# Turning q and k of three sequences by 32x32 block transposes on VectorE, from loads in blocks of 32 tokens

## Chip, core and metric

The kernel is one program on one core of a Trainium2 chip. Its time is the device time of one execution in microseconds (us). Engines are named as the profile names them: PE is TensorE's matmuls and PEld its weight loads, DVE is VectorE, ACT is ScalarE, POOL is GpSimd, SP is SyncE, from whose queue all loads and stores are issued.

## What is computed

An attention in two parts over q, k, v of shape (4 sequences, 8 heads, 576 tokens, 64), and two gated layers of 2304 tokens behind it. The reference, cut:

```python
def _attn_ref(q, k, v):                       # factor = 4, scale = 1/8
    q_d, k_d, v_d = mean over groups of 4 tokens of q, k, v
    out_d = sm_attn(q_d, k_d, v_d)            # softmax attention of 144 pooled tokens
    out_up = np.repeat(out_d, factor, axis=2)
    mask = np.abs(pos[:, None] - pos[None, :]) < factor
    scores = np.where(mask, scale * q @ k.T, -1e9)
    out_local = softmax(scores) @ v           # each token sees 7 neighbours
    return out_up + out_local

x = attn_out as (2304, 512)
h = x @ w_in;  x = (h * sigmoid(h)) @ w_out              # layer 1, 512 -> 2048 -> 512
h = x @ w2_in; out = (h * sigmoid(1.702 * h)) @ w2_out   # layer 2, the same sizes
```

The four weight arrays come as 64-bit floats.

## The kernel before

**Attention.** Two heads fill the 128 partitions, so a sequence b has 4 head pairs (hp); a half of it (288 tokens) of one head pair is a unit u, and there are 32 units. m = u // 4 is the half-sequence, 0 to 7, and b = m // 2. For each head pair of a sequence `keys_of` makes the keys: the load brings k with tokens on 96 partitions (`kraw`, two DMAs, one per head), step KT (line 1101) turns it by six TensorE transposes of fp32 against an identity into the PSUM tile `kps`, KC (line 1104, ACT) copies it to SBUF as `kT`, and KD (line 1108, DVE) sums groups of four tokens from `kps` into `kd`. For each unit, `unit` does the same with q: QT (line 1134, three transposes into `qps`), QC (line 1138, ACT, into `qT`), QD (line 1142, DVE, into `qd`). Then follow the scores SC (lines 1153 and 1159, PE, into `sl`), the softmax (LC, LS, LE, LU, LN on DVE, ACT and POOL), the transposes TP of the pooled part (line 1213, PE), a 32x32 block transpose PT of the local weights on DVE (line 1221), and the products AV with v (lines 1230 and 1236, PE). `kps` takes the tag pa2 (one PSUM buffer, shared with `sl` and a part of AV), `qps` the tag pa1 (two, shared with TP and the rest of AV). The raw tiles `kraw` and `qraw` have two buffers each.

**Layers.** The 64-bit weights of layer 1 are loaded, rebuilt as fp32 by integer steps (lines 323 to 348, the last of them, cp at line 348, a sum that stands on DVE or on POOL) and split into two fp16 parts (hi, line 376, ACT; lo, line 380, DVE). Layer 1 multiplies 12 matmuls of 288 columns per output tile: `hps` (line 691), and `ops` (line 836 for m = 0, line 808 for m = 1 to 7). Layer 2 works on blocks of 256 tokens (lines 870 and 949).

**The order.** Every piece of work is a step of a plan. The order of all steps is a table, `PLACES`: two digits per step give its place, and the steps are issued in that order on each engine's queue, where they run strictly one behind the other. The table `ON` says for some steps on which of two engines they stand: cp of layer 1 (DVE or POOL), LS and LN (the subtraction of the maximum and the scaling, lines 1182 and 1206, DVE or POOL), gs2 (sums in layer 2, lines 889 to 891, DVE or POOL). Units of the attention are threaded between the matmuls of layer 1: while layer 1 works on half-sequence m - 1 or m - 2, the units of m are made.

The transposes that the change is about, as they stand:

```python
            for c in range(2 * NBL):
                nc.tensor.transpose(T[kps][:, c // NBL, (c % NBL) * TT:(c % NBL + 1) * TT], kr[:, c].rearrange("p h d -> p (h d)"), T["ident"][:TT, :TT])
```

## Time and profile before

| | us |
|---|---|
| median of 3 runs | 930.73 (927.39 to 931.24) |
| the profiled execution | 930.08 |
| its span, first to last instruction | 928.3 |
| PE busy in the span | 866.0 (93%) |
| DVE busy | 620.6 (67%) |
| ACT busy | 474.5 (51%) |
| POOL busy | 155.6 (17%) |

The profiled execution lies 0.65 us under the median; 1.8 us of it lie outside the span. Busy shares are means over stages that differ, so the stages are read apart: the weights of layer 1 are rebuilt up to about 155 us, the attention and layer 1 share the engines up to 554 us, and layer 2 fills the rest.

### The profile page before, as it was taken

How to read it: one execution, taken by the hardware profiler on the slowest of the kernel's cores; microseconds unless marked ns; L12 is line 12 of the kernel's file. 1: busy time of each engine (PE TensorE's matmuls, PEld its weight loads, DVE VectorE, ACT ScalarE, POOL GpSimd, SP SyncE). 2: the span in 40 equal slices, each digit the busy share in tenths (PEclk: the TensorE clock that was granted, in tenths of full speed). 3: DMA queues.
4: the chain of work that ended last, by engine and by line, in shares of the span. 5: the costliest groups of instructions: out<-in, count | busy, mean ns of one | idle time of the engine just before them, and what ended most of it. 6: DMA issues, size and time to landing. Idle time of an engine off the chain costs nothing.

```text
span 928.3 us, 23669 instructions
## 1 busy us (share of the span) xinstructions
PE 866.0 (93%) x10156; PEld 709.0 (76%) x10156; DVE 620.6 (67%) x1350; ACT 474.5 (51%) x835; POOL 155.6 (17%) x180
## 2 busy tenths in 40 slices
...
GB/s 212 240 270 180 130 127 72 71 107 138 98 134 71 106 116 202 32 165 53 105 79 253 43 91 1 12 13 1 24 2 23 24 24 1 13 2 35 1 23 24
DMA packets 87388, 77.02 MB, mean 83 GB/s; under 512 B 66036, under 2 KB 72692, under 8 KB 86260
## 3 DMA queue, kind: packets, MB, share of 16 engines
...
## 4 chain that ended last, share of the span: by engine, by line
PE 63%; DVE 26%; ACT 4%; POOL 2%; issue 2%; DMA 1%; SPq 0%; POOLq 0%; ACTq 0%; DVEq 0%
PE hps L691 19%; PE ops L808 17%; PE oy L949 8%; DVE g L898 7%; PE hps L870 5%; PE oz L949 4%; DVE tg L885 3%; DVE tg L890 2%; PE ox L949 2%; PE ul L1236 2%; DVE wout L380 1%; PE sl L1159 1%; ACT g L895 1%; DVE tg L889 1%; DVE tg L891 1%
## 5 line engine op out<-in xcount | busy, mean ns | idle before, releaser
L691 PE MATMUL hps<-xhl,win 128*128 128x288 f16 x1536 | 204.0, 292 | 3.6 <-DVE tg L706 3.6
L870 PE MATMUL hps<-xhl,win 128*128 128x256 f16 x1728 | 191.4, 273 | 1.2 <-DVE tg L885 1.1
L870 PEld LDWEIGHTS <-win 128*128 128x128 f16 x1728 | 169.0, 98 | 22.0 <-issue 2.5
L691 PEld LDWEIGHTS <-win 128*128 128x128 f16 x1536 | 150.4, 100 | 44.2 <-issue 4.7
L808 PE MATMUL ops<-g,wout 128*128 128x288 f16 x1344 | 171.9, 286 | 0.0
L949 PEld LDWEIGHTS <-g 128*128 128x128 f16 x1512 | 146.5, 98 | 27.7 <-DVE g L898 8.5
L808 PEld LDWEIGHTS <-wout 128*128 128x128 f16 x1344 | 129.8, 98 | 32.5 <-issue 0.6
L882 ACT ACTIVATE tg<-hps,blk 128x512 f32<-128x512 f32 x72 | 49.2, 684 | 102.5 <-PE hps L870 99.1
L895 ACT ACTIVATE g<-tg 128x896 f16<-128x896 f32 x72 | 67.4, 945 | 49.3 <-DVE tg L891 25.4
L898 DVE SCALAR_TENSOR_TENSOR g<-tg,g 128x896 f16<-128x896 f32 x72 | 77.6, 1087 | 19.4 <-ACT g L895 19.3
L885 DVE SCALAR_TENSOR_TENSOR tg<-tg,hps 128x512 f32<-128x512 f32 x72 | 49.2, 683 | 54.6 <-ACT tg L882 54.6
L949 PE MATMUL oy<-wout,g 128*128 128x256 f16 x648 | 75.1, 272 | 0.0
L889 POOL TENSOR_TENSOR tg<-tg 128x128 f32<-128x128 f32 x17 | 8.5, 502 | 387.4 <-DVE tg L885 362.6
L348 POOL TENSOR_TENSOR cs<-cs,cz 128x512 int32<-128x512 int32 x32 | 42.1, 1327 | 135.0 <-DVE cz L336 54.3
L706 DVE SCALAR_TENSOR_TENSOR tg<-tg,hps 128x576 f32<-128x576 f32 x64 | 47.7, 748 | 23.5 <-ACT tg L703 23.1
L703 ACT ACTIVATE tg<-hps,blk 128x576 f32<-128x576 f32 x64 | 47.2, 737 | 31.1 <-PE hps L691 24.3
L713 ACT ACTIVATE g<-tg,gs 128x576 f16<-128x576 f32 x56 | 42.7, 770 | 17.5 <-DVE tg L706 17.5
L927 ACT ACTIVATE o<-oy,blk 128x256 f32<-128x256 f32 x27 | 12.8, 473 | 74.1 <-PE oy L949 74.1
L716 DVE SCALAR_TENSOR_TENSOR g<-tg,gs,g 128x576 f16<-128x576 f32 x56 | 46.9, 847 | 5.1 <-ACT g L713 5.0
L323 ACT ACTIVATE st<-st 128x512 f32<-128x512 f32 (+1 forms) x48 | 39.2, 824 | 6.2 <-DMA st<-in_moe_w_in_dram 5.9
L933 DVE SCALAR_TENSOR_TENSOR o<-oy,blk,o 128x256 f32<-128x256 f32 x9 | 4.4, 484 | 54.6 <-PE oy L949 39.4
L949 PE MATMUL oy<-wx,g 128*128 128x256 f16 x216 | 29.3, 273 | 5.1 <-DVE g L898 4.3
...
## 6 DMA issues: line engine op xcount, KB each, us to landing
...
qraw<-in_q_dram SPq DMA_DIRECT2D x64, 72.0 KB, 3.9
kraw<-in_k_dram SPq DMA_DIRECT2D x32, 144.0 KB, 5.0
...
```

What stands on the lines that cost most here:

```text
L691: nc.tensor.matmul(o, T[w][:, kc, a, fc * P:(fc + 1) * P], T[xk][:, kc, b, :T_], start=(n == 0), stop=(n == 3 * KC - 1))
L703: ACT.activation(out=T[tg], in_=T[ps][:, :, :T_], func=AF.Tanh, scale=T["a" + bk][:, c:c + 1])
L706: DVE.scalar_tensor_tensor(out=T[tg], in0=T[tg], scalar=1.0, in1=T[ps][:, :, :T_], op0=ALU.add, op1=ALU.mult)
L713: ACT.activation(out=T[g][:, 0], in_=T[tg], func=AF.Copy, scale=gs)
L716: DVE.scalar_tensor_tensor(out=T[g][:, 1], in0=T[tg], scalar=gs, in1=T[g][:, 0], op0=ALU.mult, op1=ALU.subtract)
L808: nc.tensor.matmul(o, w[:, j, a, dc * P:(dc + 1) * P], g[:, b, j % 2, :], start=(n == 0), stop=(n == 3 * NF - 1))
L870: nc.tensor.matmul(o, T[w][:, kc, a, fc * P:(fc + 1) * P], T[xk][:, kc, b, :], start=(n == 0), stop=(n == 3 * KC - 1))
L882: ACT.activation(out=four(), in_=T[ps][:, 0, :], func=AF.Tanh, scale=T["a" + bk][:, c:c + 1])
L885: DVE.scalar_tensor_tensor(out=four(), in0=four(), scalar=1.0, in1=T[ps][:, 0, :], op0=ALU.add, op1=ALU.mult)
L895: ACT.activation(out=T[g][:, 0], in_=T[tg], func=AF.Copy, scale=GS2)
L898: DVE.scalar_tensor_tensor(out=T[g][:, 1], in0=T[tg], scalar=GS2, in1=T[g][:, 0], op0=ALU.mult, op1=ALU.subtract)
L949: nc.tensor.matmul(T[bank[acc]], g[:, a, slot, :], w, start=first and p == p0 and i == 0, stop=prod in (2, 3, 4) and p == NF // 2 - 1 and ...
```

## The change

For m >= 2, that is for the sequences 1, 2 and 3 (24 of 32 units, 12 of 16 key tiles), q and k are no longer turned on TensorE. `load_tokens` loads them in four DMAs instead of two, each for one head and one half of its 64 features: 32 partitions get the tokens with the same number modulo 32, and in each partition stand blocks of 32 features, one block for each 32 tokens. A run in memory is then 32 numbers (128 bytes) where it was 64 (256 bytes). One DVE transpose of 32x32 blocks (QX, KX) turns such a tile into `qT` or `kT`; `qd` and `kd` are summed from these SBUF tiles instead of PSUM. QT, QC, KT and KC are gone for these units, and with them their PSUM tiles. `qT` loses its padding: it is 288 + 8 columns, and the scores read 32 columns from every 24th. Sequence 0 keeps the old way. Both tables are new: `PLACES` holds a new order of all steps, and in `ON` six more of the sums cp stand on POOL (12 of 16, before 6), four more of LS, three more of LN, and five fewer of the layer 2 sums gs2.

```diff
@@ -23,13 +23,14 @@
 ON = {
-    "DVE": ("sg1.in.0.2 sg1.in.1.0 sg1.in.2.2 sg1.out.1.0 sg1.out.1.2 sg1.out.2.0 sg1.out.2.2 LS0 LN1 LS2 LN2 LS3 LS5 LS7 "
...
-    "POOL": ("cp1.in.0.2 cp1.out.0.0 cp1.out.0.2 cp1.out.1.2 cp1.out.2.0 cp1.out.2.2 gs2.1.7 gs2.4.7 gs2.6.7 gs2.8.7"),
+    "DVE": ("sg1.in.0.0 sg1.in.0.2 sg1.in.1.0 sg1.in.3.0 sg1.in.3.2 sg1.out.0.0 LS1 LN1 LS2 LN3 LS6 LS8 LN12 LS15 LN16 LN18 "
...
+    "POOL": ("cp1.in.0.2 cp1.in.1.2 cp1.in.2.0 cp1.in.2.2 cp1.out.0.0 cp1.out.0.2 cp1.out.1.0 cp1.out.1.2 cp1.out.2.0 "
+             "cp1.out.2.2 cp1.out.3.0 cp1.out.3.2"),
 }
@@ -42,47 +43,46 @@
 PLACES = (
-    "0007020a03080S010U1d0o1n1K1h050b0Y1O1Z090z0M0K0Q0O0W040n0p0I0s0P1i0C131b1c1s1z1U1f1M261T2q1V2I161E1R1J1X2e2o1L2f2u2j2y2m2Q1Y2D2M2L2T2R"
...
+    "00070301040908020W1g0h1j1W1q0F0G181F200b0y0C0N0H0P100d0T1a121k141n0c0I0Y0S150V1f0l171e1b1s1d1z111D1M1H1R1N1Y1C2a2o2g2A2k2P2n2V32353839"
...
@@ -1002,9 +1002,9 @@
         for t in T["kTs"]:
             POOL.memset(t[:, 0:BAND], 0.0)
             POOL.memset(t[:, BAND + S:], 0.0)
-        T["qTs"] = [ac.tile([P, 4 * NBL, 32], F32, name=f"qT{i}") for i in range(2)]
+        T["qTs"] = [ac.tile([P, HALF + 32 - QB], F32, name=f"qT{i}") for i in range(2)]
         for t in T["qTs"]:
-            POOL.memset(t, 0.0)
+            POOL.memset(t[:, HALF:], 0.0)
         T["smr"] = [ac.tile([P, 8], F32, name=f"smr{i}") for i in range(2)]
         for t in T["smr"]:
             POOL.memset(t, 1.0)
@@ -1019,21 +1019,35 @@
 
     NU = NM * NHP
 
+    def blocked(m):
+
+        return m >= 2
+
+    def load_tokens(t, src, n, blocks):
+
+        for hh in range(2):
+            if blocks:
+                for j in range(D // 32):
+                    q = 2 * hh + j
+                    nc.sync.dma_start(out=t[32 * q:32 * q + 32, :n].rearrange("p (c e) -> p c e", e=32),
+                                      in_=src[hh].rearrange("(c p) d -> p c d", p=32)[:, :, 32 * j:32 * j + 32])
+            else:
+                nc.sync.dma_start(out=t[:TT].rearrange("p (c h d) -> p c h d", h=2, d=D)[:, :, hh], in_=src[hh].rearrange("(c p) d -> p c d", p=TT))
+
     def load_kv(b, hp):
         h = slice(2 * hp, 2 * hp + 2)
         nm = f"{b}.{hp}"
 
         def lk():
-            T["kraw" + nm] = pools["ld"].tile([TT, 2 * NBL, 2, D], F32, tag="kraw", name="kraw")
-            for hh in range(2):
-                nc.sync.dma_start(out=T["kraw" + nm][:, :, hh], in_=k[b, 2 * hp + hh].rearrange("(c p) d -> p c d", p=TT))
+            T["kraw" + nm] = pools["ld"].tile([P, S + 2 * TT], F32, tag="kraw", name="kraw")
+            load_tokens(T["kraw" + nm], [k[b, 2 * hp + hh] for hh in range(2)], S, blocked(2 * b))
 
         def lv():
             T["vraw" + nm] = pools["ld"].tile([PD, 4, BAND * D], F32, tag="vraw", name="vraw", bufs=1)
             nc.sync.dma_start(out=T["vraw" + nm], in_=v[b, h].rearrange("h (c p r) d -> p (h c) (r d)", p=PD, r=BAND))
 
         n0 = len(plan.steps)
-        add("lk" + nm, "SP", 0.44, lk, w=["kraw" + nm], alloc=[("kraw", "kraw" + nm)], mb=0.69, nd=2)
+        add("lk" + nm, "SP", 0.44, lk, w=["kraw" + nm], alloc=[("kraw", "kraw" + nm)], mb=1.0 if blocked(2 * b) else 0.69, nd=4 if blocked(2 * b) else 2)
         add("lv" + nm, "SP", 0.36, lv, w=["vraw" + nm], alloc=[("vraw", "vraw" + nm)], mb=0.33)
         if b:
             for s in plan.steps[n0:]:
@@ -1045,11 +1059,10 @@
         qk = f"qraw{u}"
 
         def f():
-            T[qk] = pools["ld"].tile([TT, NBL, 2, D], F32, tag="qraw", name="qraw")
-            for hh in range(2):
-                nc.sync.dma_start(out=T[qk][:, :, hh], in_=q[b, 2 * hp + hh, half * HALF:(half + 1) * HALF].rearrange("(c p) d -> p c d", p=TT))
-
-        add("lq" + qk, "SP", 0.44, f, w=[qk], alloc=[("qraw", qk)], mb=0.35, nd=2)
+            T[qk] = pools["ld"].tile([P, HALF + TT], F32, tag="qraw", name="qraw")
+            load_tokens(T[qk], [q[b, 2 * hp + hh, half * HALF:(half + 1) * HALF] for hh in range(2)], HALF, blocked(m))
+
+        add("lq" + qk, "SP", 0.44, f, w=[qk], alloc=[("qraw", qk)], mb=0.5 if blocked(m) else 0.35, nd=4 if blocked(m) else 2)
 
     def load_vw(b, hp):
 
@@ -1096,17 +1109,21 @@
 
         def tr():
             T[kps] = bank2("kps")
-            kr = T["kraw" + nm]
+            kr = T["kraw" + nm][:TT].rearrange("p (c h d) -> p c (h d)", h=2, d=D)
             for c in range(2 * NBL):
-                nc.tensor.transpose(T[kps][:, c // NBL, (c % NBL) * TT:(c % NBL + 1) * TT], kr[:, c].rearrange("p h d -> p (h d)"), T["ident"][:TT, :TT])
+                nc.tensor.transpose(T[kps][:, c // NBL, (c % NBL) * TT:(c % NBL + 1) * TT], kr[:, c], T["ident"][:TT, :TT])
 
         def cpy():
             ACT.copy(out=T["kTs"][hp][:, BAND:BAND + S].rearrange("p (c t) -> p c t", c=2), in_=T[kps][:, :, :HALF])
 
+        def turn():
+            DVE.transpose(out=T["kTs"][hp][:, BAND:BAND + S], in_=T["kraw" + nm][:, :S])
+
         def pool():
             T[kd] = pools["at"].tile([P, 2 * PD], F32, tag="kd", name="kd", bufs=NHP)
+            src = T["kTs"][hp][:, BAND:BAND + S].rearrange("p (c e) -> p c e", c=2) if blocked(2 * b) else T[kps][:, :, :HALF]
             DVE.tensor_reduce(out=T[kd].rearrange("p (c t) -> p c t", c=2),
-                              in_=T[kps][:, :, :HALF].rearrange("p c (t r) -> p c t r", r=BAND), axis=AX.X, op=ALU.add)
+                              in_=src.rearrange("p c (t r) -> p c t r", r=BAND), axis=AX.X, op=ALU.add)
 
         def sv():
             T[vd] = pools["at"].tile([PD, 4, D], F32, tag="vd", name="vd", bufs=NHP)
@@ -1114,9 +1131,12 @@
             POOL.tensor_tensor(out=vr[:, :, 0:2, :], in0=vr[:, :, 0:2, :], in1=vr[:, :, 2:4, :], op=ALU.add)
             POOL.tensor_tensor(out=T[vd], in0=vr[:, :, 0, :], in1=vr[:, :, 1, :], op=ALU.add)
 
-        add("KT" + nm, "PE", 0.85, tr, r=["kraw" + nm, "init"], w=[kps], alloc=[("pa2", kps, 2 * NHP * b + hp - 0.1)])
-        add("KC" + nm, "ACT", act(S), cpy, r=[kps], w=[kT], alloc=[("kT" , kT)])
-        add("KD" + nm, "DVE", dve(S), pool, r=[kps], w=[kd], alloc=[("kd", kd)])
+        if blocked(2 * b):
+            add("KX" + nm, "DVE", dve(S), turn, r=["kraw" + nm, "init"], w=[kT], alloc=[("kT", kT)])
+        else:
+            add("KT" + nm, "PE", 0.85, tr, r=["kraw" + nm, "init"], w=[kps], alloc=[("pa2", kps, 2 * NHP * b + hp - 0.1)])
+            add("KC" + nm, "ACT", act(S), cpy, r=[kps], w=[kT], alloc=[("kT" , kT)])
+        add("KD" + nm, "DVE", dve(S), pool, r=[kT if blocked(2 * b) else kps], w=[kd], alloc=[("kd", kd)])
         add("KV" + nm, "POOL", 2.1, sv, r=["vraw" + nm], w=[vd], alloc=[("vd", vd)])
 
     def unit(u):
@@ -1131,15 +1151,19 @@
         def qtr():
             T[qps] = bank1("qps")
             for c in range(NBL):
-                nc.tensor.transpose(T[qps][:, c * TT:(c + 1) * TT], T[f"qraw{u}"][:, c].rearrange("p h d -> p (h d)"), T["ident"][:TT, :TT])
+                nc.tensor.transpose(T[qps][:, c * TT:(c + 1) * TT], T[f"qraw{u}"][:TT, c * 2 * D:(c + 1) * 2 * D], T["ident"][:TT, :TT])
 
         def qcp():
             T[qT] = T["qTs"][u % 2]
-            ACT.copy(out=T[qT][:, :, 0:QB], in_=T[qps][:, :HALF].rearrange("p (s a) -> p s a", a=QB))
+            ACT.copy(out=T[qT][:, :HALF], in_=T[qps][:, :HALF])
+
+        def turn():
+            T[qT] = T["qTs"][u % 2]
+            DVE.transpose(out=T[qT][:, :HALF], in_=T[f"qraw{u}"][:, :HALF])
 
         def qpl():
             T[qd] = pools["at"].tile([P, PD], F32, tag="qd", name="qd")
-            DVE.tensor_reduce(out=T[qd], in_=T[qps][:, :HALF].rearrange("p (t r) -> p t r", r=BAND), axis=AX.X, op=ALU.add)
+            DVE.tensor_reduce(out=T[qd], in_=T[qT if blocked(m) else qps][:, :HALF].rearrange("p (t r) -> p t r", r=BAND), axis=AX.X, op=ALU.add)
 
         def scores():
 
@@ -1156,7 +1180,7 @@
                     k0 = QB * (4 * (half * NBL + bl) + i)
                     for hh in range(2):
                         r = slice(D * hh, D * hh + D)
-                        nc.tensor.matmul(T[sl][32 * i:32 * i + 32, hh, bl * 32:bl * 32 + 32], T[qT][r, 4 * bl + i, :],
+                        nc.tensor.matmul(T[sl][32 * i:32 * i + 32, hh, bl * 32:bl * 32 + 32], T[qT][r, QB * (4 * bl + i):QB * (4 * bl + i) + 32],
                                          T["kTs"][hp][r, k0:k0 + 32], start=True, stop=True, tile_position=(D * hh, 32 * i))
 
         def sd():
@@ -1253,9 +1277,12 @@
         def xmax():
             DVE.tensor_reduce(out=small(L1, m, 10 + hp), in_=T[X][:, hp, :], axis=AX.X, op=ALU.max, apply_absolute_value=True)
 
-        add(f"QT{u}", "PE", 0.43, qtr, r=[f"qraw{u}", "init"], w=[qps], alloc=[("pa1", qps, u - (0.6 if hp else 0.05))])
-        add(f"QC{u}", "ACT", act(HALF), qcp, r=[qps], w=[qT], alloc=[("qT", qT)])
-        add(f"QD{u}", "DVE", dve(HALF), qpl, r=[qps], w=[qd], alloc=[("qd", qd)])
+        if blocked(m):
+            add(f"QX{u}", "DVE", dve(HALF), turn, r=[f"qraw{u}", "init"], w=[qT], alloc=[("qT", qT)])
+        else:
+            add(f"QT{u}", "PE", 0.43, qtr, r=[f"qraw{u}", "init"], w=[qps], alloc=[("pa1", qps, u - (0.6 if hp else 0.05))])
+            add(f"QC{u}", "ACT", act(HALF), qcp, r=[qps], w=[qT], alloc=[("qT", qT)])
+        add(f"QD{u}", "DVE", dve(HALF), qpl, r=[qT if blocked(m) else qps], w=[qd], alloc=[("qd", qd)])
         add(f"SC{u}", "PE", 1.1, scores, r=[qT, qd, kT, kd], w=[sl], alloc=[("mm", sl, sl_at[u]) if u < NHP else ("pa2", sl, u)])
         add(f"DM{u}", "DVE", dve(4 * PD) + 0.2, dmax, r=[sl], w=[nmx])
         add(f"LC{u}", "DVE", 2 * dve(192), lcap, r=[sl, "cap"], w=[sc], alloc=[("sc", sc)])
```

Where the instructions stand, at three places. First PE, in the stage in which attention and layer 1 run together, around the transposes of one key tile and one unit of sequence 2 (`hps` is layer 1, `kps` and `qps` are the transposed tiles, `tps` the pooled part of the unit ahead). Before:

```order
L691 LDWEIGHTS win_2_705
L691 MATMUL hps<-xhl,win_2_705 128x288
L1101 MATMUL kps<-ident,kraw 128x96 x6
L1134 MATMUL qps<-ident,qraw 128x96 x3
L1213 MATMUL tps<-ident,pd 72x72 x4
L691 LDWEIGHTS win_3_1080
```

After, at the scores of the same unit:

```order
L691 LDWEIGHTS win_3_916
L691 MATMUL hps<-xhl,win_3_916 128x288
L1177 MATMUL sl<-kd,qd 72x144 x2
L1183 MATMUL sl<-kT_150,qT_160 32x32 x24
L691 LDWEIGHTS win_3_916
```

The nine transposes are gone from PE's row, and layer 1 stands directly on both sides of the scores.

Second DVE, at the first key tile of sequence 1, with what each instruction waits for. Before:

```order
L1254 TENSOR_REDUCE blk<-xf 128x1
L1142 TENSOR_REDUCE qd<-qps 128x72 [waits PE_49]
L1108 TENSOR_REDUCE kd<-kps 128x144 [waits PE_49]
L764 TENSOR_REDUCE blk<-rm 128x1 [waits PE_49]
L336 TENSOR_SCALAR z<-st_1053 128x1024 [waits DMAHW4_49,Activation_49]
```

After:

```order
L1245 STREAM_TRANSPOSE PT<-sc 128x192 [waits Pool_49]
L1120 STREAM_TRANSPOSE kT_148<-kraw 128x576 [waits DMAHW6_49,DMAHW7_49,DMAHW1_49,DMAHW0_49]
L1227 TENSOR_TENSOR pd<-pd,smr_165 72x288 [waits DVE_49]
L1125 TENSOR_REDUCE kd<-kT_148 128x144 [waits DVE_49]
L1197 TENSOR_TENSOR sc<-sl,cap 128x192 [waits PE_49]
L1200 TENSOR_REDUCE mx<-sc 128x6 [waits DVE_49]
```

The block transpose of `kraw` now stands in DVE's own row and waits there for four DMAs; the scaling of `pd` and the rest of the softmax of an earlier unit queue behind it.

Third POOL, while the output weights of layer 1 are rebuilt (`x_80<-x_80,z` is the sum cp, `sc<-sc,mx` is LS and `sc<-sc,smr` is LN, `vraw` and `vd` are the pooling of v). Before:

```order
L348 TENSOR_TENSOR x_80<-x_80,z 128x1024 [waits DVE_49,PE_49]
L348 TENSOR_TENSOR x_80<-x_80,z 128x1024 [waits DVE_49,PE_49,Activation_49]
L1182 TENSOR_TENSOR sc<-sc,mx 128x192 [waits DVE_49,Pool_49]
L348 TENSOR_TENSOR x_80<-x_80,z 128x1024 [waits DVE_49,PE_49]
L1114 TENSOR_TENSOR vraw<-vraw 72x4x128 [waits DMAHW3_49]
```

After:

```order
L1132 TENSOR_TENSOR vd<-vraw 72x256 [waits PE_49,Pool_49]
L348 TENSOR_TENSOR x_80<-x_80,z 128x1024 [waits Activation_49]
L348 TENSOR_TENSOR x_80<-x_80,z 128x1024 [waits DVE_49,Activation_49]
L1206 TENSOR_TENSOR sc<-sc,mx 128x192 [waits DVE_49]
L1230 TENSOR_TENSOR sc<-sc,smr_164 128x192 [waits DVE_49]
L348 TENSOR_TENSOR x_80<-x_80,z 128x1024 [waits Activation_49]
```

The sums now come in pairs, four times in this stretch, and LS and LN of the units in work queue behind them.

## Rows read from the trace of the kernel before

**Rows 1.** Windows: stretch and length, each engine's busy us, clock, DMA share, GB/s

```profile
0.00:100.00 100.00, 60.33 (x1075) 40.59 (x1076) 80.47 (x186) 69.59 (x119) 31.80 (x45) 0.98 0.89 224
100.00:155.00 55.00, 45.37 (x664) 34.34 (x662) 53.89 (x121) 44.94 (x80) 22.55 (x16) 0.94 0.53 113
155.00:554.00 399.00, 396.10 (x5139) 314.29 (x5138) 268.57 (x643) 215.75 (x442) 72.38 (x69) 1.00 0.39 108
554.00:929.00 375.00, 364.17 (x3286) 319.81 (x3283) 217.66 (x403) 144.17 (x196) 28.88 (x51) 1.00 0.04 14
```

**Rows 2.** Chain of waits, two pieces: start us, us, what ran on the path

```profile
149.43 2.64 DVE wout L380 x2
...
536.27 17.65 PE ops L808 x144
```

**Rows 3.** Timeline of PE, 211 to 219 us: start us, us (ends modelled), instruction, count

```profile
211.10 4.58 PE L808 MATMUL ops<-g,wout 128*128 128x288 f16 x36
215.52 0.66 PE L1101 MATMUL kps<-ident,kraw 96*128 96x96 f32 x6
216.02 3.11 PE L808 MATMUL ops<-g,wout 128*128 128x288 f16 x24
```

**Rows 4.** Timeline of PE, 163 us: one unit's transposes between layer 1 matmuls

```profile
163.35 0.41 PE L1134 MATMUL qps<-ident,qraw 96*128 96x96 f32 x3
163.60 1.64 PE L691 MATMUL hps<-xhl,win 128*128 128x288 f16 x12
```

**Rows 5.** Windows of line 1134 (q transposes) alone: PE, PEld, clock, DMA

```profile
100.00:155.00 55.00, 2.09 (x12) 1.35 (x12) 0.94 0.53 113
155.00:554.00 399.00, 8.43 (x60) 6.80 (x60) 1.00 0.39 108
```

**Rows 6.** Windows of line 1101 (k transposes) alone, same columns

```profile
100.00:155.00 55.00, 2.75 (x24) 2.25 (x24) 0.94 0.53 113
155.00:554.00 399.00, 5.33 (x48) 4.62 (x48) 1.00 0.39 108
```

**Rows 7.** Groups of instructions: line, engine, operation, shapes, count | busy us, mean ns | idle before

```profile
L348 POOL TENSOR_TENSOR x<-x,z 128x1024 int32<-128x1024 int32 x6 | 15.3, 2555 | 17.9 <-ACT tg L703 5.6 <-DVE z L336 4.6 <-PE kps L1101 4.4
...
L1142 DVE TENSOR_REDUCE qd<-qps 128x72 f32<-128x288 f32 x32 | 14.5, 452 | 13.0 <-PE qps L1134 11.2 <-ACT qT L1138 1.5
...
L348 DVE CUSTOM_DVE_ANT_0 x<-x,z 128x2048 uint16<-128x2048 uint16 x10 | 12.0, 1209 | 0.0
L1108 DVE TENSOR_REDUCE kd<-kps 128x144 f32<-128x576 f32 x16 | 12.0, 751 | 10.8 <-PE kps L1101 9.6 <-ACT kT L1104 1.0
L1221 DVE STREAM_TRANSPOSE PT<-sc 128x192 f32<-128x192 f32 x32 | 11.9, 371 | 1.1 <-POOL sc L1206 0.8
...
L1206 DVE TENSOR_TENSOR sc<-sc,smr 128x192 f32<-128x192 f32 x16 | 8.4, 528 | 0.2
...
L1182 DVE TENSOR_TENSOR sc<-sc,mx 128x192 f32<-128x192 f32 x14 | 5.3, 377 | 0.3
```

**Rows 8.** Timeline, all engines, 96 to 106 us: a POOL sum and one DVE form twice

```profile
96.89 3.17 POOL L348 TENSOR_TENSOR x<-x,z 128x1024 int32<-128x1024 int32 x1 [4.62 <-DVE z L336]
...
98.98 1.70 DVE L716 SCALAR_TENSOR_TENSOR g<-tg,g 128x576 f16<-128x576 f32 x1 [1.14 <-ACT g L713]
...
105.07 0.75 DVE L716 SCALAR_TENSOR_TENSOR g<-tg,g 128x576 f16<-128x576 f32 x1
```

**Rows 9.** DMA queue, 0 to 5 us: packets, MB, share of 16 engines

```profile
q1 hardware_dynamic: 2367, 0.60, 53.3%
```

**Rows 10.** DMA queue, 117 to 127 us, same columns

```profile
q1 hardware_dynamic: 4613, 1.35, 96.8%
```

**Rows 11.** DMA issues of the page: form, count, KB each, median us to landing

```profile
qraw<-in_q_dram SPq DMA_DIRECT2D x64, 72.0 KB, 3.9
kraw<-in_k_dram SPq DMA_DIRECT2D x32, 144.0 KB, 5.0
```

**Rows 12.** Timeline of SP, 231 us: four issues in one row

```profile
231.08 1.97 SPq L1067 DMA_DIRECT2D vw<-in_v_dram  x4
```

79 lines of the change are left out of this document (39 added, 40 removed), and 10 rows, old and new, of the table ON.

## The prediction

> **What bounds the kernel now.** I read the windows first, because the page's shares are means over three unlike stages. Up to 155 us DVE is the full engine, 53.89 of the last 55 us, while PE has 45.37 [rows 1]; the chain of waits runs there through DVE's splits of the weights [rows 2]. From 155 to 554 us PE is busy 396.10 of 399 us, DVE 268.57 and ACT 215.75 [rows 1], and the chain is PE's own matmuls [rows 2]. Modelled ends can make PE look fuller than it is, so I check the starts: 36 matmuls of layer 1 from 211.10 to 215.52 are 123 ns each, with nothing between them [rows 3]. PE is then truly the bound, and what leaves its row comes off the end, as long as nobody else gets late. From 554 us on PE has 364.17 of 375 us [rows 1] and no attention is left.
>
> **What PE loses.** The duration of one transpose says little, since they overlap; the start of the next instruction says it. Six transposes of a key tile hold PE from 215.52 to 216.02, 0.50 us [rows 3]; three of a unit hold it from 163.35 to 163.60, 0.25 us [rows 4]. In the PE-bound stage stand 60 transposes of q [rows 5] and 48 of k [rows 6], that is 20 units and 8 key tiles, and all belong to sequences 1 to 3. So the stage gets shorter by 20 x 0.25 + 8 x 0.50 = 5.0 + 4.0 = 9.0 us. The other 4 units and 4 key tiles (12 transposes of q, 24 of k) stand from 100 to 155 us, where PE has 9.6 us to spare [rows 1, 5, 6]; their 3.0 us I cost at nothing, because DVE covers them.
>
> **What DVE gets.** No transpose of these shapes is in the trace. The nearest row is the same operation at 192 elements, 371 ns; two reductions of 288 and 576 elements take 452 and 751 ns, so an element costs (751 - 452) / 288 = 1.04 ns [rows 7]. That gives 371 + 96 x 1.04 = 470 ns for a unit and 371 + 384 x 1.04 = 770 ns for a key tile. Bounds: the reductions of the same length below (452 and 751), and above the measured transpose with its whole time taken per element, 371 x 1.5 = 557 and 371 x 3 = 1,113 ns. I take 470 and 770, since every other row shows a fixed part. In the PE-bound stage this is 20 x 0.47 + 8 x 0.77 = 15.6 us (20.0 at the upper bounds) on an engine with 130 us free, so PE's work hides it. The copies of ACT go, and ACT waits there anyway. `qd` and `kd` are now read from SBUF; I leave their 452 and 751 ns.
>
> **The first 155 us.** Here DVE is full, so each microsecond on it counts. Up to the last split of layer 1's weights, counted in both orders, six sums cp leave DVE for POOL: 6 x 1.209 = 7.25 us less. Two LS and one LN leave it as well: 2 x 0.377 + 0.528 = 1.28 us less [rows 7]. Four key tiles and four units come: 4 x 0.77 + 4 x 0.47 = 4.96 us more. Net, DVE has 3.6 us less to do. On the other side POOL's sums hold DVE: while one ran from 96.89 for 3.17 us, a DVE instruction took 1.70 us that took 0.75 us a little later without one [rows 8]. Six more of them can cost DVE up to 6 x 0.95 = 5.7 us. The stage then ends between 3.6 us earlier and 2.1 us later; at the upper bounds of the transposes another 4 x 0.34 + 4 x 0.09 = 1.7 us come on top, 3.8 us later. With the transposes at 470 and 770 ns I take the middle of the first two, 0.8 us earlier: some of the sums will meet a DVE instruction and some won't.
>
> **Loads.** Twice the issues: four take 1.97 us of SP's queue [rows 12], so a tile costs about 1 us more there, 36 us over 36 tiles. Behind them queue layer 2's weights, which nobody needs before 554 us, and the loads of v, of which one set falls on two units or some 40 us (399 / 20 each); a microsecond per tile costs nothing against that. Twice the packets: 27,648 runs of 256 bytes become 55,296 of 128. With little else moving, a packet of mostly 256 bytes took 0.533 x 16 x 5 us / 2,367 = 18 ns [rows 9], in a crowd 0.968 x 16 x 10 us / 4,613 = 34 ns [rows 10]. If the half packet costs half, nothing is added; if it costs the same, 27,648 x 18 to 34 ns / 16 engines = 31 to 58 us of all engines. I take the middle, some 20 us; between 155 and 554 us the share of DMA is 0.39 [rows 1], so this goes into idle time, and only the landing gets later.
>
> **The other edges.** Five sums of layer 2 move from POOL to DVE, which has 157 us free there; PE idles 10.8 us in that stage and 2.9 us in the one before [rows 1]. The new order can change a part of both: nothing in the sum, 3 us each way in the range.
>
> **Sum.** Against the profiled execution of 930.1 us: 930.1 - 9.0 - 0.8 = 920.3 us. That execution lies 0.65 us under the median of the runs, so I leave it there. The mechanism's own range: 930.1 - 9.0 - 3.6 - 3.0 = 914.5 below, 930.1 - 9.0 + 3.8 + 3.0 = 927.9 above.
>
> **Rivals.** *Equal, by POOL.* The six sums are on the path, not beside it. POOL takes 2.555 us for what DVE does in 1.209 [rows 7], so each makes the weights 1.35 us later, together 8.1 us; and in pairs they stand ahead of LS and LN, on which PE's next products wait. Then the first stage ends 8.1 us later and the gain of 9.0 us is given back: 929.2 us. For it: POOL's queue is strictly in order. Against it: POOL is busy 22.55 of 55 us there, and the weights of an output tile are asked for one after the other.
>
> *Slower, by DVE's wait on loads.* Before, a late tile stopped PE at its transposes; now it stops DVE, which stands in order with the softmax and the splits behind it. The place is the eight transposes of sequence 1 before 155 us, where DVE has 1.1 us to spare. Price: landing takes 5.0 us for k and 3.9 for q [rows 11]; if it doubles with the packets and each tile is asked for at its old time, that is 4 x 5.0 + 4 x 3.9 = 35.6 us, and at half of that 930.1 - 9.8 + 17.8 = 938.1 us. It turns into a loss of over 0.5% from 15.1 us of such waits on (935.4 - 920.3). For it: DMA is at 0.53 in this stretch and at 0.97 for 10 us of it [rows 1, 10]. Against it: the first key tile of sequence 1 is loaded ahead of six loads of layer 1's output weights, and its transpose stands early in DVE's row, so it was not placed at the last moment.
>
> [...]
>
> *Faster still, by the order.* If the 3.0 us of transposes before 155 us had been on the path after all, DVE's 3.6 us come in full, and the new order also saves the 3.0 us of the other edges, the time is 930.1 - 9.0 - 3.0 - 3.6 - 3.0 = 911.5 us. That the transposes don't really leave PE is excluded: the order has 36 rows fewer there.
>
> **Chances and range.** The forecast has 0.68, the equal case 0.17, the slower one 0.10, the faster still 0.05. A measurement of this kernel tells about 0.5% from no change, 926.1 to 935.4 us around the median. Faster by more than that: nearly all of the forecast and the faster case, 0.73. Within: the equal case and the upper edge of the forecast, 0.18. Slower: 0.09. The range leaves out the slower case and a part of the equal one: from 912.5, between the forecast's lower bound and the faster case, to 929, the equal case.
>
> **What will show it.** Right: no matmuls on `kps` and `qps` after some 90 us, layer 1's matmuls at 123 ns on both sides of the scores, a PE-bound stage of about 390 us where it was 399, DVE transposes of 0.47 and 0.77 us, and the start of layer 2's matmuls about 10 us earlier. Wrong: the first stage ending after 158 us with waits of DVE on `kraw` or `qraw`, or on POOL; or PE idling more than 6 us between 155 and 545 us because scores wait for `qT` or `kT`.

## The result, and the profile after

The changed kernel takes 907.5 us (median; 904.4 to 908.4) against 929.1 us (927.2 to 931.2) for the kernel before, run beside it: a ratio of 0.976, 95% interval 0.973 to 0.980. That is 13 us less than the 920.3 us forecast and under the range of 912.5 to 929 us. The profiled execution took 907.1 us, its span is 905.3 us.

I cut both traces at the same two events: the start of the last product of `o1` for m = 0 (line 836), and the first product of layer 2 (line 870). Windows of the kernel before, then of the changed one; the columns are those of [rows 1]:

```profile
0.00:160.60 160.60, 111.30 (x1783) 79.45 (x1784) 138.62 (x320) 114.93 (x199) 54.35 (x60) 0.97 0.74 178
160.60:558.16 397.56, 394.66 (x5125) 313.08 (x5123) 268.46 (x631) 219.51 (x445) 72.38 (x69) 1.00 0.39 109
558.16:928.30 370.14, 360.01 (x3252) 316.49 (x3249) 213.50 (x400) 140.01 (x193) 28.88 (x51) 1.00 0.04 14
```

```profile
0.00:153.24 153.24, 105.30 (x1747) 75.32 (x1748) 133.76 (x324) 112.17 (x192) 69.00 (x70) 0.96 0.69 191
153.24:536.69 383.45, 383.45 (x5016) 302.57 (x5013) 276.30 (x647) 206.11 (x416) 74.21 (x72) 1.00 0.39 111
536.69:905.30 368.61, 359.57 (x3254) 316.82 (x3251) 219.93 (x418) 140.77 (x193) 22.97 (x36) 1.00 0.04 14
```

The start is 7.4 us shorter, the stage of attention and layer 1 14.1 us, layer 2 1.5 us: together 23.0. In the middle stage PE had 2.9 us without work; now it has none. Its timeline, which answers to [rows 3], has the scores between layer 1's products and no transposes:

```profile
210.22 0.47 PE L1177 MATMUL sl<-kd,qd 64*72 64x144 f32 x4
210.62 0.62 PE L1183 MATMUL sl<-kT,qT 64*32 64x32 f32 x48
211.17 4.58 PE L808 MATMUL ops<-g,wout 128*128 128x288 f16 x36
215.59 0.28 PE L758 MATMUL rm<-blk,ones 128*128 128x4 f32 x2
```

The 36 products from 211.17 to 215.59 are 123 ns each, as before.

The groups of the changed kernel that answer to [rows 7] (count | busy us, mean ns | idle before them):

```profile
L1162 DVE STREAM_TRANSPOSE qT<-qraw 128x288 f32<-128x288 f32 x24 | 11.0, 460 | 1.8 <-DMA qraw<-in_q_dram 1.7
L1120 DVE STREAM_TRANSPOSE kT<-kraw 128x576 f32<-128x576 f32 x12 | 9.1, 761 | 0.9 <-PE sl L1183 0.9
...
L348 POOL TENSOR_TENSOR x<-x,z 128x1024 int32<-128x1024 int32 x12 | 31.1, 2590 | 32.0 <-PE ul L1260 14.1
```

The transposes take 460 and 761 ns, where I had 470 and 770, and those of q wait for their loads 1.7 us in all. The loads answer to [rows 11] (KB each, median us from issue to landing):

```profile
kraw<-in_k_dram SPq DMA_DIRECT2D x48, 72.0 KB, 3.1
qraw<-in_q_dram SPq DMA_DIRECT2D x96, 36.0 KB, 2.0
```

and the queue of the whole span, before and after (packets, MB, share of 16 engines):

```profile
q1 hardware_dynamic: 87284, 75.51, 30.4%
```

```profile
q1 hardware_dynamic: 116084, 75.52, 29.2%
```

Nearly 29,000 packets more, and the time on the DMA engines fell, from 0.304 x 928.3 = 282 to 0.292 x 905.3 = 264 us each.

### The profile page after: what moved, and what is told of

The parts are those of the page before. It is cut to its first block, busy times and chain, and to the rows that moved or that the text cites. A ratio compares the mean times of both kernels' runs of the same rounds, so it can differ in the third digit from the quotient of the medians.

```text
span 905.3 us, 23450 instructions
## 1 busy us (share of the span) xinstructions
PE 848.3 (94%) x10012; PEld 694.7 (77%) x10012; DVE 630.0 (70%) x1387; ACT 459.0 (51%) x800; POOL 166.2 (18%) x178
## 4 chain that ended last, share of the span: by engine, by line
PE 65%; DVE 25%; ACT 3%; DMA 3%; issue 2%; POOL 1%; SPq 1%; DVEq 0%; ACTq 0%; POOLq 0%
PE hps L691 19%; PE ops L808 18%; PE oy L949 9%; DVE g L898 6%; PE hps L870 6%; PE oz L949 4%; DVE tg L885 4%; DVE tg L890 2%; PE ox L949 2%; PE ul L1260 2%; DMA st<-in_moe_w_in_dram 2%; DVE tg L891 2%; DVE tg L889 2%; PE ops L836 1%; PE sl L1183 1%
## 5 line engine op out<-in xcount | busy, mean ns | idle before, releaser
L691 PE MATMUL hps<-xhl,win 128*128 128x288 f16 x1536 | 199.3, 289 | 0.0
L348 POOL TENSOR_TENSOR x<-x,z 128x1024 int32<-128x1024 int32 x12 | 31.1, 2590 | 32.0 <-PE ul L1260 14.1
```

What stands on the lines that cost most here:

```text
L348: eng.tensor_tensor(out=s, in0=s, in1=zget(), op=ALU.add)
L691: nc.tensor.matmul(o, T[w][:, kc, a, fc * P:(fc + 1) * P], T[xk][:, kc, b, :T_], start=(n == 0), stop=(n == 3 * KC - 1))
```

## The experiments

The table has all runs. "Start" is the time of the first cut, DVE's busy time in it beside its idle time (the rest of the start); "stage" is the time between the cuts. The ratio is to the kernel before, run beside each. All are read from one profiled execution each, but for the median and the ratio.

| kernel | median us | ratio (95%) | start | DVE busy / idle | stage |
|---|---|---|---|---|---|
| before | 929.1 | | 160.6 | 138.6 / 22.0 | 397.6 |
| changed | 907.5 | 0.976 (0.973 to 0.980) | 153.2 | 133.8 / 19.5 | 383.4 |
| e1_turn | 933.1 | 1.004 (1.002 to 1.005) | 163.6 | 142.4 / 21.3 | 397.1 |
| e2_sums | 933.5 | 1.005 (1.004 to 1.007) | 163.1 | 141.6 / 21.5 | 396.2 |
| e3_order | 953.8 | 1.027 (1.025 to 1.029) | 163.9 | 131.1 / 32.9 | 417.5 |
| e4_sumsback | 908.9 | 0.978 (0.976 to 0.981) | 154.2 | 137.0 / 17.2 | 383.4 |
| e5_lead | 926.6 | 0.996 (0.994 to 0.997) | 163.1 | 141.8 / 21.3 | 392.1 |
| e6_start | 914.8 | 0.984 (0.981 to 0.986) | 152.1 | 133.6 / 18.5 | 390.0 |
| e7_rest | 917.7 | 0.986 (0.984 to 0.989) | 160.7 | 140.4 / 20.3 | 383.4 |
| e8_late | 913.1 | 0.981 (0.979 to 0.983) | 152.4 | 133.7 / 18.7 | 388.3 |
| e9_loads | 932.0 | 1.003 (1.002 to 1.005) | 175.5 | 133.6 / 41.9 | 383.4 |
| e10_seq1 | 929.3 | 1.001 (0.999 to 1.002) | 165.8 | 130.5 / 35.3 | 394.2 |
| e11_loads | 922.2 | 0.993 (0.991 to 0.994) | 167.7 | 139.6 / 28.1 | 383.6 |
| e12_twice | 916.2 | 0.987 (0.985 to 0.989) | 159.5 | 141.1 / 18.4 | 385.5 |
| e13_pool | 928.8 | 1.000 (0.999 to 1.001) | 160.6 | 139.6 / 21.0 | 397.6 |
| e14_sums16 | 908.4 | 0.977 (0.976 to 0.979) | 153.9 | 135.5 / 18.4 | 383.4 |
| e15_ls | 905.7 | 0.975 (0.973 to 0.976) | 154.6 | 132.6 / 22.0 | 383.4 |
| e16_short | 922.8 | 0.992 (0.991 to 0.994) | 158.7 | 130.6 / 28.0 | 393.9 |
| e17_short2 | 927.0 | 0.998 (0.997 to 0.999) | 159.4 | 138.5 / 20.9 | 393.9 |

Where an edit is a new order, its diff is written in the names of the steps, cut to the row of one engine around one unit or key tile; the others are moved alike.

### One part alone

**e1_turn**, the transposes and loads without the new order. DVE around unit 16, against the kernel before:

```diff
+KX2.0
 KD2.0
+QX16
 QD16
 am1.3
```

> The transposes and the blocked loads alone: the order of all steps and the table ON are those of the kernel before; KX and QX stand on DVE directly ahead of KD and QD, the transposes on PE and the copies on ACT are gone, and four loads stand a few places later. Theory A, the new order made what my sum lacked (the start up to the last product of o1 for m = 0, 7.4 us; the stall at 366 us, about 4.8 us; layer 2, 1.5 us): the PE-bound stage loses 9.3 us, the start ends between 160.6 and 165 us since DVE gets 5 us more, the stall stays, and the time is 930.1 - 9.3 + 0 to 4 = 921 to 925 us. Theory B, the transposes made it all (PE, ACT and the PSUM tiles that they hold are free, so all goes earlier): the start ends at about 153 us, and the time is 907 to 912 us. Theory C, the sums cp made the gain of the start: 921 to 925 us here too, told apart from A by the next run.

The time is 933 us, above all three theories: no gain at all. The transposes did leave PE, whose busy time in the stage falls by 8.4 us, and it idles 10.8 us where it idled 2.9. Window of that stage, and what PE waited for in it (us, times, longest):

```profile
163.63:560.77 397.14, 386.30 (x5018) 303.47 (x5016) 283.74 (x659) 207.99 (x417) 72.20 (x69) 1.00 0.39 109
```

```profile
PE hps L690 <- DVE tg L705: 5.4, 2, 3.7
PE sl L1176 <- DVE kd L1124: 2.4, 2, 1.6
PE sl L1176 <- DVE qd L1165: 2.1, 2, 1.7
```

Theory A had the 9.3 us as certain; they are not. DVE comes to `QX` late, and scores and gates behind it are late on PE. One unit shows it: its QX starts 1.1 us ahead of its scores, and these wait for the pooling `qd` behind QX.

```profile
201.73 0.46 DVE L1161 STREAM_TRANSPOSE qT<-qraw 128x288 f32<-128x288 f32 x1
202.83 0.47 PE L1176 MATMUL sl<-kd,qd 64*72 64x144 f32 x4 [1.67 <-DVE qd L1165]
```

**e2_sums**, the sums cp alone, in the kernel before:

```diff
-    "POOL": ("cp1.in.0.2 cp1.out.0.0 cp1.out.0.2 cp1.out.1.2 cp1.out.2.0 cp1.out.2.2 gs2.1.7 gs2.4.7 gs2.6.7 gs2.8.7"),
+    "POOL": ("cp1.in.0.2 cp1.in.1.2 cp1.in.2.0 cp1.in.2.2 cp1.out.0.0 cp1.out.0.2 cp1.out.1.0 cp1.out.1.2 cp1.out.2.0 "
+             "cp1.out.2.2 cp1.out.3.0 cp1.out.3.2 gs2.1.7 gs2.4.7 gs2.6.7 gs2.8.7"),
```

> The kernel before with one thing changed: the 12 sums cp of the changed kernel stand on POOL, where it had 6. Theory C, DVE is full in the start and each microsecond taken from it comes off the end: 6 x 1.21 = 7.3 us less on DVE, the start ends at 153 to 155 us, the time is 923 to 925 us. Theory of my prediction, POOL's sums hold DVE: between 5.7 us of that given back, so 2 to 4 us gained or nothing, 926 to 930 us. The rival that called it equal, POOL's longer sum lies on the path: 6 x 1.35 us later, 936 to 938 us. Theory A, the order made the gain of the start: within 2 us of the kernel before, 928 to 932 us.

4 us slower by the medians, which none of the four theories had, and 1.1 us by the profiled executions; the start ends 2.5 us later. DVE lost 7.3 us of sums and was busy 3.0 us longer, so other instructions grew by some 10 us; I had bounded that at 5.7. The smallest show it best. The row of line 1168 in the start of the kernel before, then the same operation in e2_sums:

```profile
L1168 DVE TENSOR_SCALAR nm<-nm 72x2 f32<-72x2 f32 x12 | 3.2, 264 | 0.4
```

```profile
L1169 DVE TENSOR_SCALAR nm<-nm 72x2 f32<-72x2 f32 x12 | 6.4, 537 | 0.4
```

**e3_order**, the order alone. PE around unit 8, against the changed kernel; PSUM holds KT1.0 back to 95 places behind where KX1.0 stood:

```diff
 AV7
+KT1.0
+QT8
 SC8
```

> The order and the table ON of the changed kernel with the transposes on PE: KT and KC stand where KX stood, QT and QC where QX stood, and what PSUM doesn't allow there stands later. The loads are the old ones. Theory A, the order made what my sum lacked: the start ends at 153 to 156 us (DVE has 5 us less than in the changed kernel, PE 3 us more), the PE-bound stage has its 9.3 us of transposes again, and the time is 907.5 + 9.3 = 917 us, up to 920 us for the steps that stand later. Theory B, the transposes made it all: 925 to 932 us, with the start at 160 us.

The slowest of all. PE's timeline (start us, us, what), with a wait behind the transposes:

```profile
348.43 0.66 PE L1101 MATMUL kps<-ident,kraw 96*128 96x96 f32 x6
348.93 0.41 PE L1134 MATMUL qps<-ident,qraw 96*128 96x96 f32 x3
351.37 0.47 PE L1153 MATMUL sl<-kd,qd 64*72 64x144 f32 x4 [2.03 <-DVE kd L1108]
```

The copy and the pooling have no time left between transposes and scores. So the two halves of the change, as they are, need each other. An order made anew for transposes on PE wasn't tried, so what a new order alone could give stays open.

**e4_sumsback**, the six sums back on DVE in the changed kernel:

```diff
-    "POOL": ("cp1.in.0.2 cp1.in.1.2 cp1.in.2.0 cp1.in.2.2 cp1.out.0.0 cp1.out.0.2 cp1.out.1.0 cp1.out.1.2 cp1.out.2.0 "
-             "cp1.out.2.2 cp1.out.3.0 cp1.out.3.2"),
+    "POOL": ("cp1.in.0.2 cp1.out.0.0 cp1.out.0.2 cp1.out.1.2 cp1.out.2.0 cp1.out.2.2"),
```

> The changed kernel with one thing put back: only the 6 sums cp of the kernel before stand on POOL, the other 10 on DVE. Theory C, DVE is full in the start: 6 x 1.21 = 7.3 us more, the start ends at 158 to 161 us, the time is 913 to 915 us. Theory of my prediction, POOL's sums hold DVE by up to 0.95 us each: 1.6 to 7.3 us more, 909 to 915 us. Theory A, the order and not the sums: within 2 us of the changed kernel, 905.5 to 909.5 us.

1.4 us more than the changed kernel's median, within what can be told (the intervals overlap): the sums are not the gain. DVE was busy 3.3 us longer, and the start ended 1.0 us later.

### The lead

**e5_lead**: DVE around unit 16, against e1_turn:

```diff
+KX2.0
...
 XA14
+QX16
...
 cg2.in.1.0
+KD2.0
...
 XM15
-KX2.0
-KD2.0
-QX16
 QD16
```

> As e1_turn (old order, old table ON, transposes on DVE), but from unit 10 on the transposes stand well ahead of the scores that need them: QX 40 places ahead of where QT stood, KX 60 ahead of KT, QD and KD 12 places ahead of their old place, and their loads 60 and 80 places earlier. In e1_turn the scores of a unit began some 2.3 us after its QX began, in the changed kernel some 14 us. Theory of the lead: the 9.3 us of transposes are really off PE, but in e1_turn DVE, which works in order, comes to QX late and PE waits for it (the matmuls of h1 grew by 8.7 us); with the lead the stage behind the start goes from 397 to 386 to 390 us and the time from 933 to 921 to 926 us. Theory that DVE has no room for the 15 us of transposes in that stage, wherever they stand: 930 to 935 us.

926.6 us, 6.6 less than e1_turn, just past the slow end of what the lead should give; the stage, 392.1 us, is 2 us above its forecast. From the start of QX to the first product of its scores a unit now has 14.0 us (median of 24), in e1_turn 2.5 and in the changed kernel 13.7 (single units from 1.5 to 33). In the changed kernel the scores of 210.22 us above have this QX ahead of them, 7.7 us earlier:

```profile
202.56 0.47 DVE L1162 STREAM_TRANSPOSE qT<-qraw 128x288 f32<-128x288 f32 x1
```

PE's waits for `kd` and `qd` are gone; what stays is

```profile
PE hps L690 <- DVE tg L705: 5.0, 4, 2.3
```

**e6_start** and **e7_rest** put the two halves of the order together the other way. The rule that made both orders:

```diff
 place of a step, e6_start:
+up to the last o1 of m = 0: as in the changed kernel
+behind it: as in e5_lead
 place of a step, e7_rest:
+up to the last o1 of m = 0: as in e1_turn
+behind it: as in the changed kernel
```

> As e5_lead, but up to the last product of o1 for m = 0 the order is that of the changed kernel, and the steps of the table ON that belong there (sg1, cp, LS and LN of the units 0 to 11) are the changed kernel's too. If the start's gain is the order of the start alone: the start ends at 153 to 155 us where it ended at 163.6 in e1_turn, and the time is 8 to 10 us under that of e5_lead (911 to 918 us if e5_lead gives 921 to 926). If the start hangs on what comes behind it: at most 3 us under e5_lead.

> The other half: up to the last product of o1 for m = 0 order and table as in e1_turn (the old ones with transposes on DVE), behind it those of the changed kernel. If the parts add up: the start ends at 163 to 164 us, the stage behind it takes 383 to 386 us and layer 2 368.6, together 917 to 920 us. If the short stage of the changed kernel (no stall at 366 us) depends on the way the start leaves the buffers: a stage of 390 us or more, 924 us or more.

The changed parts keep their times. The changed order's start takes 152 to 153 us in front of either stage, and its stage 383.4 to 383.6 us behind whatever start, here and in five other rows of the table (e4, e9, e11, e14, e15). The old start does not add up as well: 160.7 us in e7_rest, where e1_turn has 163.6 and 163 to 164 were foreseen; why isn't known.

**e8_late** takes the lead away in the changed kernel; DVE around unit 16:

```diff
-KX2.0
...
-KD2.0
...
-QX16
...
 PT15
+KX2.0
+KD2.0
-QD16
 cs2.in.0.3
-KD2.1
+QX16
+QD16
 XM14
```

> The changed kernel with the lead taken away: from unit 12 on KX, KD, QX and QD stand directly ahead of the scores in the order (13, 12, 10 and 9 places), as in e1_turn; all else is the changed kernel's. Theory of the lead: the stage from 153 us on grows by 5 to 12 us, 912 to 920 us. Theory that the rest of the order and not the lead makes the short stage: within 2 us of the changed kernel, 905.5 to 909.5 us.

The stage grows by 4.9 us, just under the 5 to 12 foreseen, with 3.5 us from QX to the scores (median). Not all of it need be the lead: PE also waited 1.6 us for loads of v, which it didn't in the changed kernel, and the new places of the transposes change when the buffers of the loads ahead of them come free.

### What sets the start

**e9_loads** puts back the order of the loads alone, **e11_loads** puts the new loads ahead of the old start of e7_rest. SP's first rows, e9_loads against the changed kernel:

```diff
-lv0.0
 lqqraw1
 lk0.0
 lqqraw0
-lv0.1
+ldst1in.0.2
 lk0.1
 ldst1in.0.0
-ldst1in.1.0
-ldst1in.0.2
+lv0.0
```

> The changed kernel with one queue put back: on SP the loads of the start stand in the order of the kernel before (there the second half of layer 1's first input weights comes ahead of the first half, and the sums' and later weights behind more of q, k and v); all other engines keep the changed order. If the start's 7.4 us come from the order of the loads: the start ends at 157 to 161 us, the time is 911 to 915 us, perhaps more since the work on the engines now expects other weights first. If they come from the order on the engines: within 2 us of the changed kernel, 905.5 to 909.5 us.

> e7_rest (old order up to the last product of o1 for m = 0, the changed one behind) with the loads of the start in the changed kernel's order; no other engine's order is touched. If the loads make the start's gain: it ends at 153 to 156 us where it ended at 160.7, the time is 910 to 913 us. If the order on the engines makes it: 160 to 162 us, 915 to 919 us.

Both lose, 22.2 us of the start against the changed kernel and 7.0 against e7_rest, and both runs are slower than the figures of either theory. Neither "the loads" nor "the engines" makes it: a queue's order is worth something beside the others that were fitted to it. DVE's work in e9_loads is that of the changed kernel; its idle time doubles, with these waits (in the changed kernel 2.5 us and nothing):

```profile
DVE x L331 <- ACT st L323: 12.3, 3, 8.8
DVE kT L1120 <- DMA kraw<-in_k_dram: 9.6, 1, 9.6
```

**e10_seq1** turns sequence 1 the old way in the changed order:

```diff
-        return m >= 2
+        return m >= 4
```

> The changed kernel with only sequences 2 and 3 turned on DVE; sequence 1 is loaded and turned the old way, KT, KC, QT and QC standing where KX and QX stood or as soon after that as PSUM allows. I had costed the 36 transposes of sequence 1 that lie in the start at nothing, because DVE covers them. By that and with 5 us less on DVE in the start: it ends at 150 to 154 us, and the stage behind it gets 8 x 0.25 = 2.0 us longer at most (the units 12 to 15 alone 1.0), 905 to 911 us. If the PSUM tiles and the copies on ACT that go with the old way hold up the start, as e3_order suggests (its start ended at 163.9 us with the changed order): 160 to 164 us, 916 to 920 us or more.

The start grows by 12.5 us, although DVE has 3.3 us less to do, and the stage by 10.7 us, where 2 at most were foreseen. In the same view of the start KD now waits for the copies of `kT` as well; its wait for `kps` was there in the changed kernel (last row), for the key tiles of sequence 0:

```profile
DVE kd L1125 <- ACT kT L1117: 7.1, 3, 4.8
DVE kd L1125 <- PE kps L1114: 4.2, 2, 3.5
```

```profile
DVE kd L1125 <- PE kps L1114: 4.8, 2, 3.4
```

So the 36 transposes that I had costed at nothing are more than a load on PE: with them back DVE idles 15.8 us more, 6.5 of it in these two waits. In the program they are a link in a chain, since `kps` needs the only buffer of pa2 and KD needs `kps`; that this chain makes the loss is argued, not shown. Like e3_order, the run puts the old way into an order that was not made for it.

**e12_twice**:

```diff
+            for _ in range(2):
                 DVE.transpose(out=T[qT][:, :HALF], in_=T[f"qraw{u}"][:, :HALF])
```

> The changed kernel with each transpose KX and QX done twice, one right behind the other: 24 x 0.46 + 12 x 0.76 = 20.2 us more on DVE, of which 4 x (0.46 + 0.76) = 4.9 us lie in the start. If the transposes are hidden behind PE in the stage from 153 us on, as I had costed them, and DVE is full in the start: the start ends 3 to 5 us later, the stage takes 383 to 385 us, the time is 910 to 913 us. If DVE has slack in the start too: within 2 us of the changed kernel. If DVE has no room in the later stage: 15 us more there, up to 927 us.

As foreseen for a DVE that hides them in the stage (2.0 us more, with DVE busy 13.4 us longer) and not in the start: it ends 6.2 us later, more than the 3 to 5 I wrote, with DVE busy 7.3 us longer. So the time, 916.2 us, lies above the 910 to 913 foreseen.

**e14_sums16** and **e15_ls** try what DVE's small steps are worth:

```diff
-    "POOL": ("cp1.in.0.2 cp1.in.1.2 ...
+    "POOL": ("cp1.in.0.0 cp1.in.0.2 cp1.in.1.0 cp1.in.1.2 ...   (all 16; e14_sums16)
-    "DVE": ("sg1.in.0.0 ... sg1.out.0.0 LS1 LN1 LS2 LN3 LS6 LS8 LN12 ...
+    "DVE": ("sg1.in.0.0 ... sg1.out.0.0 LN12 ...   (e15_ls)
```

> The changed kernel with all 16 sums cp on POOL (it has 12). If what counts in the start is DVE's work: 4 x 1.21 = 4.8 us less, the start ends up to 4.8 us earlier, 902.7 to 905 us, the fastest yet. From e4_sumsback, where six sums back on DVE cost 1.4 us: 0.2 us each, so 906.5 us. If POOL's sums now hold DVE or lie on the path of the weights, as in e2_sums: 909 to 915 us.

> The changed kernel with six small softmax steps of the start (LS of the units 1, 2, 6 and 8, LN of 1 and 3) moved from DVE to POOL: 6 steps of 0.35 to 0.53 us, 2.4 us less on DVE in the start, 4.5 us more on POOL. If DVE's work alone counts: 905 us. If each of them was put on DVE because the scores' chain waits for it: 909 to 915 us.

Both are the changed kernel's time within what can be told (the intervals overlap), so neither decides between its theories; e15_ls's median lies near the 905 us of "DVE's work alone counts", and its profiled execution, 908.5 us, was the slowest of five. In the profiled executions, work that leaves DVE comes back as longer instructions (e14_sums16: 4.8 us of sums gone, DVE busy 1.7 us longer) or as idle time (e15_ls). That need not contradict e12_twice: work added into a chain of waits counts, work taken away at another place can leave a hole.

### The stall at 366 us

In the kernel before, POOL works without a break from 367.92 to 373 us, and PE's `hps` products stand still for 1.97 us up to 374 us. Behind the wait they run at a granted clock of 0.51 (374.14 to 377.10 us; 12 products in 3.04 us, elsewhere 1.64):

```profile
374.14 3.04 PE L691 MATMUL hps<-xhl,win 128*128 128x288 f16 x12 [1.97 <-DVE tg L706]
```

In the changed kernel there is no such stall.

**e13_pool** moves POOL's work there; POOL's row, against the kernel before:

```diff
-cp2.out.0.0
-cp2.out.0.1
 KV3.3
+cp2.out.0.0
+cp2.out.0.1
```

> The kernel before with one place changed: the two POOL sums of layer 2's weights that ran from 367.92 us (cp, 2.50 us, then the sums of v behind them until 373 us), and the two ACT steps that read them, stand behind the gate steps of the next output tiles, and the sums of v ahead of them. Theory: POOL's 5 us in a row held DVE (1.11, 1.66 and 1.51 us for three instructions there), so that tg came late and PE stood 1.97 us and then ran a while at the lower clock; with the sums apart the stall of about 4.5 us between 360 and 380 us goes, in full or in good part, and the time is 925 to 928.5 us. Rival, the stall is DVE's own in-order work (softmax, pooling) ahead of tg and POOL has no part in it: it stays, 929 to 931 us.

The stall stays (PE waits 2.21 us for `tg`), but the run doesn't speak for the rival: POOL still worked in one piece, from 367.45 to 372.24 us. Before (the first pair of rows, POOL and DVE) and in e13_pool (the second pair):

```profile
367.92 2.50 POOL L348 TENSOR_TENSOR cs<-cs,cz 128x512 int32<-128x512 int32 x2 [15.93 <-DVE cz L336]
...
369.37 1.66 DVE L716 SCALAR_TENSOR_TENSOR g<-tg,gs,g 128x576 f16<-128x576 f32 x1
```

```profile
369.74 2.50 POOL L347 TENSOR_TENSOR cs<-cs,cz 128x512 int32<-128x512 int32 x2
...
369.16 3.69 DVE L715 SCALAR_TENSOR_TENSOR g<-tg,gs,g 128x576 f16<-128x576 f32 x1
```

**e16_short** and **e17_short2** take that work away instead:

```diff
-            eng.tensor_tensor(out=s, in0=s, in1=zget(), op=ALU.add)
+            w = 8 if nm in ("2.out.0.0", "2.out.0.1") else s.shape[-1]
+            eng.tensor_tensor(out=s[:, :w], in0=s[:, :w], in1=zget()[:, :w], op=ALU.add)
...
-            POOL.tensor_tensor(out=vr[:, :, 0:2, :], in0=vr[:, :, 0:2, :], in1=vr[:, :, 2:4, :], op=ALU.add)
+            w = 2 if nm == "3.3" else D
+            POOL.tensor_tensor(out=vr[:, :, 0:2, :w], in0=vr[:, :, 0:2, :w], in1=vr[:, :, 2:4, :w], op=ALU.add)
```

(e16_short has 512 in place of `s.shape[-1]`, which also halves layer 1's sums.)

> The kernel before with POOL's work near 368 us cut: two sums of layer 2's weights (the first two column blocks of w2_out) add only 8 of 512 columns, and the first of the two sums of v of the last key tile only 2 of 64 features; all the rest, the order too, is as before. POOL's 5.1 us there become some 1.5. In e13_pool these same operations, in another order but still in a row, held a gate step of DVE for 3.69 us, and the stall stayed. Theory, POOL's run holds DVE: the three instructions of DVE that took 1.11, 1.66 and 1.51 us take 0.2, 0.82 and 0.44, PE's wait of 1.97 us goes, 360 to 380 us loses 2 to 4.5 us, and the time is 925 to 928 us. Rival, DVE's own work in its order makes the stall: it stays, 929 to 931 us.

> As e16_short, but with layer 1's sums whole: e16_short had cut these too, to 512 of their 1,024 columns, which it was not meant to do. Left out are only two sums of layer 2's weights (8 of 512 columns are added) and a part of the last sum of v (2 of 64 features). If the stall near 368 us is POOL's hold on DVE: the start ends at 160.6 us as before, the products o1 of m = 4 end 3.5 us sooner behind those of m = 3 (55 us where it was 58.6), the time is 925 to 927 us. If e16_short lost the stall through its shorter start: 929 to 931 us.

In both the stage is 393.9 us, 3.65 less, and all of it lies between the last products of m = 3 and m = 4: up to there e17_short2 is ahead by the 1.2 us of its start, behind it by 4.8. The gate step that took 1.66 us in the kernel before, in e17_short2, and its PE:

```profile
367.30 0.77 DVE L717 SCALAR_TENSOR_TENSOR g<-tg,gs,g 128x576 f16<-128x576 f32 x1
...
366.43 6.15 PE L692 MATMUL hps<-xhl,win 128*128 128x288 f16 x48
```

48 products without a gap: the stall was POOL's hold on DVE. 1.97 us of wait and 1.4 us at the lower clock make most of its 3.65 us. Two things stay open: e17_short2's start is 1.2 us shorter than that of the kernel before, with the same work, and its median gains 1.5 us (927.0, at the edge of the forecast) where the profiled execution gains 4.8. So what the stall costs a typical execution of the kernel before isn't known.

e16_short tells something of the start, too. With layer 1's sums halved DVE is busy 8.0 us less, and the start ends only 1.9 us sooner; DVE idles the rest.

## Why the prediction was wrong, point by point

| term | forecast | measured |
|---|---|---|
| transposes off PE, middle stage | -9.0 | -9.3 (what they held PE before) |
| start, up to the last o1 of m = 0 | -0.8 | -7.4 |
| other edges of the middle stage | 0 | -4.8 |
| layer 2 | 0 | -1.5 |
| sum, profiled executions | -9.8 | -23.0 |

**What PE loses: right in size, with a condition that got no price.** From start to start q's transposes held PE 5.26 us and k's 4.02 in that stage of the kernel before, and since the changed kernel's PE has no idle time there, all of it came off. The prediction says "as long as nobody else gets late", but its argument that PE's work hides the transposes compared DVE's 15.6 us with its 130 us of free time, as a sum. e1_turn has about as much free time and gets nothing, since DVE must reach QX before PE reaches the scores; with a lead of 14 us in the old order the stage is 5.0 us shorter than e1_turn's (e5_lead), and the changed kernel's loses 4.9 us without its lead (e8_late). So the term came true, for about half of it at least, because the new order has a lead of 13.7 us, which I hadn't looked for in it; that it came out whole is luck. The signs named for it came: no products on `kps` or `qps` behind 87 us, layer 1's at 123 ns, transposes of 0.46 and 0.76 us.

**The first 155 us: the step that failed.** I took DVE as full, counted what joins and leaves it (3.6 us less), set half of POOL's hold against it, and came to -0.8 us where the start lost 7.4. The balance was not far off: of the 7.4 us, 4.9 are less work on DVE and 2.5 less idle time. In the terms of the sum, POOL's hold, put at some +2.8 us, was no net cost in the new order, and idle time, put at nothing, fell by 2.5. What failed behind both is the rule that DVE's work sets the end. The start ends with DVE's work plus its idle time, and work taken from DVE mostly turned into idle time (e16_short: 8.0 us less work, 1.9 us less time), while the order of the loads alone moved the end by 22 us with the same work (e9_loads). What made 7.4 us is the changed order together with sequence 1 on DVE; without either the start takes 160.7 to 165.8 us (e1_turn, e7_rest, e3_order, e10_seq1). Which single wait in it counts stays open.

**The price of POOL's hold** was too low for the old order: 0.95 us for each of six sums in [rows 8], some 10 us in all in e2_sums. In the changed order the forms that stand as often on DVE in both starts are together about 1 us shorter, although twelve sums stand on POOL instead of six. They still hold DVE there: with six of them back on it (e4_sumsback) its other work is 4 us shorter, 0.7 us for each. What the traces show of it: the gate of 0.8 us took 3.69 us under POOL's 4.8 us (e13_pool), while in the start of e2_sums `tg` and the reduction `kd` kept their times of the kernel before (746 and 745 ns, before 744 and 746). What tells the two kinds apart no run shows.

**Other edges: not nothing.** 3.65 of the 4.8 us are that hold at one place (e17_short2). Of the other 1.2 us, 0.9 are the one other wait of PE in that stage of the kernel before, which the changed kernel doesn't have:

```profile
PE sl L1153 <- DVE kd L1108: 0.9, 1, 0.9
```

Layer 2's 1.5 us had no run of their own, but they go with the new order and its table `ON`: layer 2 takes 368.7 to 369.6 us in the runs with the changed order there (e7_rest, e3_order) and 370.1 to 370.4 with the old one (e1_turn, e6_start).

**Loads: no price, as forecast, but the size was wrong.** I allowed some 20 us more of all DMA engines and put them into idle time; the total fell by 18. In the trace's packet records a 128-byte packet of the changed kernel took 12.7 ns in the mean (55,296 of them). One of 256 bytes took 19.3 in the same kernel (33,784) and 24.7 in the kernel before (61,432, q and k among them). Two halves thus cost 1.3 times a whole by the first and about the same by the second; the records don't name the tensor of a packet, so which is the fairer pair stays open.

**The rivals.** *Equal, by POOL*: its 8.1 us didn't come. In the old order the six sums cost 2.5 us of the start and 4 us in all (e2_sums), in the new one nothing that can be told (e4_sumsback). *Slower, by waits on loads*: 1.7 us in the changed kernel; its mechanism is real, one wait of 9.6 us in e9_loads, where the loads don't fit. *Faster still, by the order*: the right side, at 0.05 and with too small a price. My range took the order for an edge of 3 us, though the diff said that it was new from end to end.
